# Attention and a feed-forward layer on one core: turned blocks written at the end of a slot, the product with v at its slot's end

## Chip, cores and metric

The kernel runs on one core of a Trainium2 chip. The metric is the device time of one execution in microseconds (us). Engines are named as the profile names them: PE (TensorE, matrix products), PEld (its weight loads), DVE (VectorE), ACT (ScalarE), POOL (GpSimd) and SP (SyncE, which here issues every transfer).

## Reference

8 batches, 8 heads, 576 positions, head size 64; model width 512. An attention with a decay on the scores, then a normalised feed-forward layer with a residual, all in float32:

```python
scores = scale * np.matmul(q, k.transpose(0, 1, 3, 2))
cum = np.cumsum(np.log(np.clip(f, 0.0001, 1.0)), axis=-1)
scores = np.where(causal, -1e9, scores + cum[:, :, :, None] - cum[:, :, None, :])
attn = np.exp(scores - scores.max(-1)); attn = attn / (attn.sum(-1) + 1e-9)
x = np.matmul(attn, v)                      # heads side by side: (8, 576, 512)
xn = (x - mu) / np.sqrt(var + 1e-6) * g_ln
out = x + np.maximum(xn @ w_ch1, 0.0) @ w_ch2
```

## The kernel before

**Two lanes of work, one list of slots.** The 64 heads are walked one after the other, each in four slots, one for each group of query rows: t = 1, 2, 3, 4 with 192, 320, 448 and 576 keys (the slot t = 1 also does the 64x64 corner, tile 0). I call them t1 to t4; the slot after t4 is t1 of the next head. In each slot, besides its attention work, one unit of the feed-forward layer runs: `mm1` (lines 691 to 693, twelve products into `h`) and `mm2` (lines 713 to 715, six products into `acc`, for the unit of the slot before). There are 288 such units; those that the slots do not hold run after the last head.

**Two forms of a head.** Heads 0 to 15 (`full`) are done with plain float32 products. Heads 16 to 63 split every operand in a high and a low part. Their probabilities must be transposed before the product with v, and this is done without PE. These are the pieces that matter here:

- `Q`, `S`, `e`, `B`: scores on PE (384, 385); score plus mask with the row minimum on DVE (425); exponential on ACT (436); on DVE the reciprocal of the row sum (441, 442) and on POOL the multiplication by it (443).
- `T`, one slot after the scores: `turn` transposes 32x32 blocks of the probabilities on DVE (461, 463) into a buffer `pb`. There is one `pb` for the whole kernel.
- `write` (471): in the slots t3 and t1 one transfer brings `pb` with two slots' blocks to DRAM (`pd`): 128x768 floats for query groups 1 and 2, 128x1152 for groups 3 and 4. Before the change it is issued right behind `T`.
- `V` (`read`, 482): in the slots t4 and t2 four transfers read `pd` back in the transposed order, into `pt`; one buffer for each of the two sizes.
- `H`, `G` (498, 502), `l` (506), `o` (513): in the slots t2 and t4, four slots after the scores, ACT copies the high part `ph`, DVE and POOL subtract it to get the low part; `o`, on POOL, overwrites `pt`.
- `A` (606): in the slots t1 and t3, PE multiplies both parts with `vv`. `F` (647) and `a` (658) bring the result to SBUF on ACT and DVE, and for every second head a transfer writes it to DRAM (660).
- `k`: in t1 the raw keys of the next head are split (ACT 342, POOL 345), in t3 its raw queries (ACT 350, POOL 356). Both come through one buffer `raw`, loaded by line 325. In a slot t1 the queries are loaded over the keys, and in a slot t3 the keys of the head behind them over the queries: each load waits until POOL has subtracted from the old content. In t3 `load_v` (332) follows it. `values_high` (362, DVE) and `values_low` (365, POOL) split v.

**What sets the order.** No scheduler: `ORDERS` (line 51) holds one letter for each piece, and the loop over the slots runs the pieces in the order of the letters. Each engine executes its instructions in the order in which they were issued, and so does SP with its transfers: a transfer that waits holds back all behind it. `M` and `N` are `mm1` and `mm2`, `m` the low part of their hidden values (704), `R` the loads and splits of the next token chunk, `D` the loads of raw q, k and v, `b` and `L` the small statistics of a chunk. A chunk of 256 tokens ends every 16 slots, with two transfers to the output (792).

Of the kernel before, what the change touches and what calls it, by code (L numbers as in the profile page):

```python
# [15 lines left out]
B, H, S, D = 8, 8, 576, 64  # L16
# [5 lines left out]
C = 256  # L22
# [27 lines left out]

ORDERS = [
    (0, "WwQsSthAeMrgFBmlLNPaRf"),
    (37, "WwkQSTstAMhPeHlgNFGrxfmBoVDLRba"),
    (66, "kQSTAHeVGFtlahBoMPrxmNbRLD"),
]


# [1 line left out]
def attn_moe(ctx: ExitStack, tc: tile.TileContext, qk, v, f, g, w1, w2, out):  # L59
# [304 lines left out]
    def values_low(h):  # L364
        nc.gpsimd.tensor_tensor(
            out=h.vv[:, :, 1, :], in0=h.vr, in1=h.vv[:, :, 0, :].bitcast(F32), op=ALU.subtract
        )
# [100 lines left out]
    def write(h, t):  # L468
        w = (6 if t == 2 else 9) * 32
        pd = dram.tile([P, 4 * w], F32, tag=f"pd{t}", bufs=2, name=f"pd{t}_{h.n}")  # L470
        nc.sync.dma_start(out=pd, in_=turned[0][:, : 4 * w])
        h.pd = getattr(h, "pd", {})
        h.pd[t] = pd
# [177 lines left out]
    def finish_add(h):  # L651
        po, w, c0 = h.o
        b, hh = divmod(h.n, H)
        pr, j = divmod(hh, 2)
        g1, xs = c0 == 0, h.xs
        js = slice(64 * j, 64 * j + 64)
        if not h.full:
            nc.vector.tensor_tensor(out=xs[js, :], in0=po[0:64, :w], in1=h.tmp[js, :w], op=ALU.add)  # L658
        if j == 1:
            nc.sync.dma_start(out=(xd1 if g1 else xd2)[b][P * pr : P * pr + P, :], in_=xs)  # L660
# [198 lines left out]

    slots = [(n, t) for n in range(B * H) for t in (1, 2, 3, 4)]  # L860
    nu = len(slots)
    slots += [None] * (DONE + 1)
    hd = {}

    def start_head(n):
# [12 lines left out]
    for u, slot in enumerate(slots):  # L878

        def before(k):  # L880
            return slots[u - k] if u >= k else None
# [5 lines left out]
        for back in (LAG + 1, DONE):  # L887
            if before(back) is not None and before(back)[1] in (2, 4) and hd[before(back)[0]].full == (back == LAG + 1):
                av, av_t = hd[before(back)[0]], before(back)[1]
        want = moe.can(wp.ready()) and u >= FIRST_MOE  # L890

        def tiles(h, t):
# [4 lines left out]
        def piece(c):  # L897
            tu = before(LAG)
            if tu is not None and not hd[tu[0]].full:
                tu = None  # L900
            late = before(HIGH)
            if late is not None and (hd[late[0]].full or late[1] in (1, 3)):
                late = None
            due_read = before(READ)
            if due_read is not None and (hd[due_read[0]].full or due_read[1] in (1, 3)):
                due_read = None
            past = before(1)
            if past is not None and hd[past[0]].full:
                past = None
            if c == "t" and tu is not None:  # L910
                transpose_unit(hd[tu[0]], tu[1])
            elif c == "h" and tu is not None:
                transposed_hi(hd[tu[0]], tu[1])
            elif c == "T" and past is not None:
                for i in [1, 0] if past[1] == 1 else [past[1]]:
                    turn(hd[past[0]], i)
                if past[1] in (2, 4):
                    write(hd[past[0]], past[1])
            elif c == "V" and due_read is not None:
                read(hd[due_read[0]], due_read[1])  # L920
            elif c == "H" and late is not None:
                high_first(hd[late[0]], late[1])
            elif c == "G" and late is not None:
                high_rest(hd[late[0]], late[1])
            elif c == "l" and late is not None:
                low_first(hd[late[0]], late[1])
            elif c == "k":
                two = before(2)
                if two is not None and two[1] == 4 and not hd[two[0]].full:
                    values_low(hd[two[0]])  # L930
                if slot is not None and n + 1 >= NFULL and n + 1 < B * H and t in (1, 3):
                    (keys_high if t == 1 else queries_high)(hd[n + 1])
                    (keys_low if t == 1 else queries_low)(hd[n + 1])
            elif c == "x" and slot is not None and n + 1 >= NFULL and n + 1 < B * H and t == 3:
                queries_copy(hd[n + 1])
            elif c == "o" and late is not None:
                low_rest(hd[late[0]], late[1])
            elif c == "Q" and slot is not None:
                for i in tiles(h, t):
                    qk_mm(h, i)  # L940
            elif c == "A" and av is not None:
                av_unit(av, av_t)
            elif c == "S" and slot is not None:
                for i in tiles(h, t):
                    softmax_a(h, i)
            elif c == "e" and slot is not None:
                for i in tiles(h, t):
                    softmax_e(h, i)
            elif c in FILL:
                wp.fill(FILL[c])  # L950
            elif c == "s":
                wp.sums()
                if u == LAG:
                    busy(WARM[2])
            elif c == "F" and av is not None:
                finish(av)
            elif c == "a" and av is not None:
                finish_add(av)
            elif c == "r" and want:
                moe.first_high()  # L960
            elif c == "R":
                moe.limit = min(NCHUNK, max(0, min(u - LAG - 1, max(4 * NFULL, u - DONE))) // (4 * H) * S // C)
                moe.rest()
            elif c == "b":
                rows_stats(moe.cur)
            elif c == "L":
                run_later(RSTD)
            elif c == "M" and want:
                moe.first()
            elif c == "B" and slot is not None:  # L970
                for i in tiles(h, t):
                    softmax_b(h, i)
            elif c == "m" and want:
                moe.first_low()
            elif c == "W":
                due = 1 + min(u, W_CHANGE) / W_SLOTS + max(0, u - W_CHANGE) * W_TICKS
                while not wp.done() and wp.tick_no <= due:
                    wp.tick()
            elif c == "N":
                moe.second()  # L980
            elif c == "P":
                prep()
            elif c == "D":
                next_raw()
# [23 lines left out]

        def prep():

            if before(1) is not None and before(1)[1] == 4 and not hd[before(1)[0]].full:
                values_high(hd[before(1)[0]])
            if slot is not None:
                if t == 1 and n + 1 < NFULL:
                    start_head(n + 1)
                if t == LAG + 1 and h.full:
                    load_v(hd[n + 1])
# [51 lines left out]
```

## Time and profile before

| | |
|---|---|
| Median of 3 runs | 1284.99 us (1283.32 to 1291.8) |
| The profiled execution | 1285.22 us, span 1283.2 us |
| Granted PE clock, mean | 0.987 |
| Busy share of the span | PE 90%, PEld 80%, DVE 60%, ACT 50%, POOL 46% |
| Transfers | 185.35 MB on SP's queue, 48.5% of 16 DMA engines' span |

The split heads fill the span from about 240 to 1070 us; then feed-forward units alone run until the end. A row of groups or of the timeline names the engine, the line, the tile written and the tiles read, and the shape; the number in brackets is the idle time of the engine ahead of it and what ended it. A row of the waits gives, for one engine and line, whom it waited for: us in total, how often, and the longest. `SPq` is SP's queue of transfers; its time for a transfer is that of issuing it, not of the transfer. A timeline of several engines is printed in order of time; where it was asked for one engine, rows of others are missing.

### The profile page before, as it was taken

To read this page: it belongs to the slowest core of one execution; us is meant where nothing else is said; L and a number is where in the kernel's file an instruction comes from. 1 tells how busy PE (TensorE), PEld (TensorE's weight loads), DVE (VectorE), ACT (ScalarE), POOL (GpSimd) and SP (SyncE) were. 2 spreads that over 40 slices of the span, in tenths; PEclk is the share of its full clock that TensorE was granted. 3 is DMA by queue.
4 is the path that set the end of the run, shared out by engine and by line. 5 is a ranking of instruction groups with operands and counts; after the bars stand their busy time and mean duration, and the time that the engine had idled before them with its cause. 6 is when DMAs were issued, how large, how long until landed. Compare 5 with 4: busy or idle time off the path is not lost. (4 is left out here: it accounts for less than half of the span.)

```text
span 1283.2 us, 24610 instructions
## 1 busy us (share of the span) xinstructions
PE 1159.3 (90%) x7648; PEld 1025.9 (80%) x7648; DVE 770.7 (60%) x2706; ACT 646.2 (50%) x1744; POOL 594.3 (46%) x870
## 2 busy tenths in 40 slices
PE   8889999888988888988888988889888889999998
PEld 6657888778887787878787878788787879999997
DVE  6777774576757576666667676766666672222222
ACT  6886665455555555545555555555455542111111
POOL 3454454465556565555655565655555541000000
PEclk9999999999999999999999999999999999999999
DMA  6555532656656555647565656556565642110100
GB/s 182 161 146 159 159 83 66 187 165 184 185 169 178 161 172 186 195 153 203 174 182 175 200 166 179 157 186 180 170 189 175 187 149 60 45 38 18 50 25 25
DMA packets 165169, 186.91 MB, mean 146 GB/s; under 512 B 45488, under 2 KB 131504, under 8 KB 165040
## 3 DMA queue, kind: packets, MB, share of 16 engines
q1 hardware_dynamic: 165040, 185.35, 48.5%
q8 instruction: 61, 1.00, 0.3%
q14 instruction: 68, 0.56, 0.2%
HBM read 118.93 MB, written 66.36 MB: 144 GB/s over the span
## 5 line engine op out<-in xcount | busy, mean ns | idle before, releaser
L443 POOL TENSOR_SCALAR p<-p,st 64x64 f32<-64x64 f32 (+4 forms) x320 | 169.6, 535 | 434.6 <-DVE st L442 196.7
L691 PE MATMUL h<-x,w1h 128*128 128x256 f32 x1152 | 336.0, 292 | 0.4 <-DVE st L425 0.4
L692 PE MATMUL h<-x,w1h 128*128 128x256 f32 x1152 | 328.8, 285 | 0.0
L693 PE MATMUL h<-x,w1l 128*128 128x256 f32 x1152 | 328.8, 285 | 0.0
L436 ACT ACTIVATE p<-p,st 64x64 f32<-64x64 f32 (+4 forms) x320 | 179.1, 560 | 264.4 <-DVE st L425 244.9
L704 DVE SCALAR_TENSOR_TENSOR hh<-h,hh 128x256 fp32r<-128x256 f32 x288 | 121.7, 422 | 229.1 <-ACT hh L699 227.5
L713 PE MATMUL acc<-w2h,hh 128*128 128x512 f32 x576 | 230.7, 401 | 0.0
L714 PE MATMUL acc<-w2l,hh 128*128 128x512 f32 x576 | 229.8, 399 | 0.0
L699 ACT ACTIVATE hh<-h 128x256 fp32r<-128x256 f32 x288 | 109.6, 380 | 237.7 <-PE h L693 236.1
L715 PE MATMUL acc<-w2h,hh 128*128 128x512 f32 x576 | 227.0, 394 | 0.0
L691 PEld LDWEIGHTS h<-x,w1h 128*128 128x128 f32 x1152 | 221.6, 192 | 5.5 <-issue 0.9
L692 PEld LDWEIGHTS h<-x,w1h 128*128 128x128 f32 x1152 | 222.9, 193 | 2.5
L693 PEld LDWEIGHTS h<-x,w1l 128*128 128x128 f32 x1152 | 223.1, 194 | 0.0
L425 DVE CUSTOM_DVE_ANT_0 p<-s,mask 64x64 f32<-64x64 f32 (+4 forms) x320 | 130.5, 422 | 82.4 <-PE s L385 76.6
L513 POOL TENSOR_TENSOR pt<-pt,ph 128x384 fp32r<-128x384 f32 x96 | 149.5, 1558 | 6.1 <-ACT ph L502 6.1
L606 PE MATMUL o<-pt,vv 128*64 128x256 f32 (+1 forms) x288 | 48.9, 278 | 101.4 <-POOL pt L513 97.8
L715 PEld LDWEIGHTS acc<-w2h,hh 128*128 128x128 f32 x576 | 109.7, 190 | 25.3
L713 PEld LDWEIGHTS acc<-w2h,hh 128*128 128x128 f32 x576 | 111.3, 193 | 14.5 <-ACT ph_full L568 0.2
L606 PEld LDWEIGHTS o<-pt,vv 128*64 128x64 f32 x288 | 29.6, 135 | 115.4 <-POOL pt L513 115.4
L714 PEld LDWEIGHTS acc<-w2l,hh 128*128 128x128 f32 x576 | 111.0, 193 | 12.0
L658 DVE TENSOR_TENSOR xs<-o,ot 64x320 f32<-64x320 f32 x96 | 43.2, 450 | 125.8 <-ACT ot L647 125.8
L776 POOL TENSOR_SCALAR sv<-sv 128x2 f32<-128x2 f32 x18 | 3.9, 215 | 188.9 <-DVE sv L760 187.7
(87 smaller groups left out, 2013.9 us busy)
## 6 DMA issues: line engine op xcount, KB each, us to landing
raw<-in_qk_dram SPq DMA_DIRECT2D x96, 288.0 KB
pd<-pb SPq DMA_DIRECT2D x48, 576.0 KB
pd<-pb SPq DMA_DIRECT2D x48, 384.0 KB
wr<-in_w_dram SPq DMA_DIRECT2D x32, 512.0 KB
pt<-pd SPq DMA_DIRECT2D x96, 144.0 KB
pt<-pd SPq DMA_DIRECT2D x96, 112.0 KB
vr<-in_v_dram SPq DMA_DIRECT2D x64, 160.0 KB
out_dram<-xt SPq DMA_DIRECT2D x36, 256.0 KB
```

The lines of the kernel that those rows point to most:

```text
L425: nc.vector.tensor_tensor_reduce(out=pt[:m, a:z], in0=sp, in1=mask[:m, off + a : off + z], scale=-SCALE, scalar=3.0e38 if i == 0 else st[: ...
L436: nc.scalar.activation(pt[:m, :w], pt[:m, :w], AF.Exp, bias=st[:m, i : i + 1], scale=-1.0, accum_out=st[:m, 2:3])
L443: nc.gpsimd.tensor_scalar(out=pt[:m, :w], in0=pt[:m, :w], scalar1=st[:m, 3:4], scalar2=1.0, op0=ALU.mult, op1=ALU.mult)
L513: nc.gpsimd.tensor_tensor(out=pt[:, :, z:, :], in0=pt[:, :, z:, :].bitcast(F32), in1=ph[:, :, z:, :].bitcast(F32), op=ALU.subtract)
L691: mm(ph, w1h[:, k, fs], c.x[k][:, 0, :], start=(k == 0), stop=False)
L692: mm(ph, w1h[:, k, fs], c.x[k][:, 1, :], start=False, stop=False)
L693: mm(ph, w1l[:, k, fs], c.x[k][:, 0, :], start=False, stop=(k == KT - 1))
L699: nc.scalar.activation(h[:, 0, :], c.ph, AF.Relu)
L704: nc.vector.scalar_tensor_tensor(out=h[:, 1, :], in0=ph, scalar=0.0, in1=h[:, 0, :].bitcast(F32), op0=ALU.max, op1=ALU.subtract)
L713: mm(c.acc[i], h[:, 0, ts_], w2h[:, j, :], start=(j == 0), stop=False)
L714: mm(c.acc[i], h[:, 0, ts_], w2l[:, j, :], start=False, stop=False)
L715: mm(c.acc[i], h[:, 1, ts_], w2h[:, j, :], start=False, stop=(j == FT - 1))
```

## The change

From slot 67 on (head 16, t4) the letters stand in another order, and three pieces move by a slot:

- The product with v, `A`, moves from behind the scores to the end of the slot, behind `M` and `N`. Its results `F` and `a` move to the next slot, so from t1 and t3 to t2 and t4 (`fin`).
- `V` moves from the middle of its slot to behind `D`.
- The write of `pb`, so far part of `T`, becomes a piece of its own, `d`, the last of the slot (the row of slot 37 has it too, since head 16's first slots fall under that row).
- v's split moves one slot: `values_high` from t1 to t2, `values_low` from t2 to t3. The limit of the feed-forward lane moves by a slot, and one empty slot is added at the end.

```diff
 ORDERS = [
     (0, "WwQsSthAeMrgFBmlLNPaRf"),
-    (37, "WwkQSTstAMhPeHlgNFGrxfmBoVDLRba"),
-    (66, "kQSTAHeVGFtlahBoMPrxmNbRLD"),
+    (37, "WwkQSTstAMhPeHlgNFGrxfmBoVDLRbad"),
+    (67, "kQSTHeGFtlahBoMNAPrxmbRLDVd"),
 ]
...
-    slots += [None] * (DONE + 1)
+    slots += [None] * (DONE + 2)
...
+        fin = av if av is not None and av.full else None
+        if before(DONE + 1) is not None and before(DONE + 1)[1] in (2, 4) and not hd[before(DONE + 1)[0]].full:
+            fin = hd[before(DONE + 1)[0]]
...
-                if past[1] in (2, 4):
-                    write(hd[past[0]], past[1])
+            elif c == "d" and past is not None and past[1] in (2, 4):
+                write(hd[past[0]], past[1])
...
-                two = before(2)
-                if two is not None and two[1] == 4 and not hd[two[0]].full:
-                    values_low(hd[two[0]])
+                three = before(3)
+                if three is not None and three[1] == 4 and not hd[three[0]].full:
+                    values_low(hd[three[0]])
...
-            elif c == "F" and av is not None:
-                finish(av)
-            elif c == "a" and av is not None:
-                finish_add(av)
+            elif c == "F" and fin is not None:
+                finish(fin)
+            elif c == "a" and fin is not None:
+                finish_add(fin)
...
-                moe.limit = min(NCHUNK, max(0, min(u - LAG - 1, max(4 * NFULL, u - DONE))) // (4 * H) * S // C)
+                moe.limit = min(NCHUNK, max(0, min(u - LAG - 1, max(4 * NFULL, u - DONE - 1))) // (4 * H) * S // C)
...
-            if before(1) is not None and before(1)[1] == 4 and not hd[before(1)[0]].full:
-                values_high(hd[before(1)[0]])
+            if before(2) is not None and before(2)[1] == 4 and not hd[before(2)[0]].full:
+                values_high(hd[before(2)[0]])
```

**PE in a slot t1**, before: the product with v (`o`, lines 606; `ph` the high part, `pt` the low one) stands between the scores `s` and the unit of the feed-forward layer.

```order
L384 MATMUL s_0_0_6328<-hi_6075 64x128
L385 MATMUL s_0_0_6328<-kl_6076,xq_2840 64x128
L606 MATMUL o_4_6340<-ph_29_6276,vv_6130 128x256 x4
L606 MATMUL o_4_6340<-ph_29_6276,vv_6130 128x128
L606 MATMUL o_4_6340<-pt_29_6161,vv_6130 64x256 x3
L606 MATMUL o_4_6340<-pt_29_6161,vv_6130 64x128
L691 MATMUL h_0_6362<-x_0_5897,w1h 128x256
```

After, in the same slot:

```order
L713 MATMUL acc_1_5492<-w2h,hh_15_6304 128x512
L714 MATMUL acc_1_5492<-w2l,hh_15_6304 128x512
L715 MATMUL acc_1_5492<-w2h,hh_15_6304 128x512
L606 MATMUL o_4_6369<-ph_29_6272,vv_6183 128x256 x4
L606 MATMUL o_4_6369<-ph_29_6272,vv_6183 128x128
L606 MATMUL o_4_6369<-pt_29_6199,vv_6183 64x256 x3
L606 MATMUL o_4_6369<-pt_29_6199,vv_6183 64x128
L384 MATMUL s_2_0_6386<-hi_6075 128x320
```

The 18 products of lines 691 to 715 now stand ahead of it, and the scores of the next slot behind it.

**SP's transfers from a slot t1 to the next slot t3**, before, with what each waits for (`DMAHW` and a number: the completion of an earlier transfer, eight counters that the transfers take in turn; an engine's name: an instruction of that engine):

```order
L471 DMA pd_30_6338<-pb 128x1152 [waits DMAHW2_49,DVE_49]
L660 DMA xb_158<-xs_320_6107 128x256 [waits DMAHW3_49,DVE_49]
L792 DMA out_dram<-xt_0_6068 128x512 [waits DMAHW4_49,DVE_49]
L792 DMA out_dram<-xt_1_6194 128x512 [waits DMAHW5_49,DVE_49]
L325 DMA raw_0_6390<-in_qk_dram 128x576 [waits DMAHW6_49,Pool_49]
L482 DMA pt_30_6405<-pd_30_6338 32x4x288 [waits DMAHW7_49,DMAHW2_49,PE_49]
L482 DMA pt_30_6405<-pd_30_6338 32x4x288 [waits DMAHW0_49]
L482 DMA pt_30_6405<-pd_30_6338 32x4x224 [waits DMAHW1_49]
L482 DMA pt_30_6405<-pd_30_6338 32x4x224
L471 DMA pd_31_6450<-pb 128x768 [waits DMAHW3_49,DVE_49]
L325 DMA raw_1_6489<-in_qk_dram 128x576 [waits DMAHW6_49,DMAHW4_49,Pool_49]
L332 DMA vr_6491<-in_v_dram 128x320 [waits DMAHW5_49]
```

After:

```order
L792 DMA out_dram<-xt_0_6063 128x512 [waits DMAHW2_49,DVE_49]
L792 DMA out_dram<-xt_1_6188 128x512 [waits DVE_49]
L325 DMA raw_0_6382<-in_qk_dram 128x576 [waits DMAHW4_49,Pool_49]
L471 DMA pd_30_6384<-pb 128x1152 [waits DMAHW5_49]
L660 DMA xb_158<-xs_320_6155 128x256 [waits DMAHW6_49,DVE_49]
L482 DMA pt_30_6434<-pd_30_6384 32x4x288 [waits DMAHW7_49,DMAHW5_49,PE_49]
L482 DMA pt_30_6434<-pd_30_6384 32x4x288 [waits DMAHW0_49]
L482 DMA pt_30_6434<-pd_30_6384 32x4x224 [waits DMAHW1_49]
L482 DMA pt_30_6434<-pd_30_6384 32x4x224 [waits DMAHW2_49]
L325 DMA raw_1_6483<-in_qk_dram 128x576 [waits DMAHW4_49,DMAHW3_49,Pool_49]
L332 DMA vr_6485<-in_v_dram 128x320 [waits DVE_49]
L471 DMA pd_31_6487<-pb 128x768 [waits DVE_49]
```

Each write of `pb` (471) stood ahead of the load of `raw` (325) in its slot and now stands behind it, in t3 behind the load of v too.

**DVE in a slot t2**, before (the 320-key query group; `p_1` and `p_1_177` are the probabilities of the slot before, which `T` turns into `pb`):

```order
L425 ISA p_2_6396,st_2_6397<-s_2_0_6393,mask 128x320 [waits PE_49]
L425 ISA st_2_6397 128x1
L461 STREAM_TRANSPOSE pb<-p_1_6331 128x2x32 [waits DMAHW2_49,Pool_49]
L463 STREAM_TRANSPOSE pb<-p_1_6331 128x4x32
L461 STREAM_TRANSPOSE pb<-p_1_177 64x2x32 [waits Pool_49]
L506 TENSOR_TENSOR ph_30_6402<-pt_30_6279,ph_30_6402 64x4x96 [waits DMAHW6_49,DMAHW5_49,Activation_49]
L441 TENSOR_SCALAR st_2_6397<-st_2_6397 128x1 [waits Activation_49]
```

After:

```order
L425 ISA p_2_6389,st_2_6390<-s_2_0_6386,mask 128x320 [waits PE_49]
L425 ISA st_2_6390 128x1
L461 STREAM_TRANSPOSE pb<-p_1_6331 128x2x32 [waits DMAHW5_49,Pool_49]
L463 STREAM_TRANSPOSE pb<-p_1_6331 128x4x32
L461 STREAM_TRANSPOSE pb<-p_1_177 64x2x32 [waits Pool_49]
L506 TENSOR_TENSOR ph_30_6395<-pt_30_6315,ph_30_6395 64x4x96 [waits DMAHW6_49,Activation_49]
L658 TENSOR_TENSOR xs_320_6155<-o_4_6369,ot_320_6399 64x256 [waits Activation_49]
L441 TENSOR_SCALAR st_2_6390<-st_2_6390 128x1
```

Before and after, the first transposition waits for the completion of the write of `pb` that was issued in the slot t1 (`DMAHW2` in the one, `DMAHW5` in the other), since it overwrites what that write reads. `a` (658) has come in ahead of the reciprocal's first step (441).

## The prediction

> **What bounds the kernel now.** I read the stretches of 50 us first. A row of the stretches gives the stretch, its length, then the busy time of PE, PEld, DVE, ACT and POOL with their instructions, the granted clock, the transfers' share and GB/s.
>
> ```profile
> 600.00:650.00 50.00, 43.29 (x288) 39.19 (x287) 34.23 (x124) 26.49 (x70) 30.46 (x44) 1.00 0.55 168
> 1100.00:1150.00 50.00, 50.00 (x327) 45.52 (x326) 11.65 (x27) 8.68 (x23) 2.75 (x14) 1.00 0.12 34
> ```
>
> PE is the bound, wholly so in the tail (50.00 of 50). Between 240 and 1070 us it idles 6.7 of 50 us at a clock of 1.00, so something else ends last there at some point of each slot. The waits name it:
>
> ```profile
> PE o L606 <- POOL pt L513: 97.8, 64, 2.5
> DVE xs L658 <- ACT ot L647: 125.8, 96, 3.8
> SPq L471 <- DVE pb L463: 266.5, 93, 6.2
> SPq L325 <- POOL kl L345: 31.9, 22, 5.6
> SPq L325 <- POOL hi L356: 31.1, 23, 2.2
> DVE pb L461 <- DMA pd<-pb: 3.5, 3, 2.2
> ```
>
> PE waits 97.8 us for POOL's low part `o` ahead of the product with v, nearly all that it idles in this stage. The lower four rows matter for the change. SP waits 266.5 us for the transposed blocks: it arrives early at each write of `pb`, and the write goes as soon as the blocks exist. Only behind it SP waits for POOL, to load `raw`. And DVE hardly ever waits for the write (3.5 us in all) when it transposes into `pb` again a slot later.
>
> One head without chunk work, from the timelines of single engines:
>
> ```profile
> 642.04 0.24 DVE L461 STREAM_TRANSPOSE pb<-p 128x64 f32<-128x64 f32 x1
> 643.74 0.53 POOL L443 TENSOR_SCALAR p<-p,st 128x320 f32<-128x320 f32 x1 [2.43 <-DMA pt<-pd]
> 644.24 1.01 POOL L513 TENSOR_TENSOR pt<-pt,ph 128x384 fp32r<-128x384 f32 x1
> 645.33 1.43 POOL L356 TENSOR_TENSOR hi<-raw,hi 64x576 fp32r<-64x576 f32 x1
> 646.01 0.34 SPq L471 DMA_DIRECT2D pd<-pb  x1
> 647.78 0.38 SPq L325 DMA_DIRECT2D raw<-in_qk_dram  x1
> 650.00 0.24 DVE L461 STREAM_TRANSPOSE pb<-p 128x64 f32<-128x64 f32 x1
> 651.70 0.75 POOL L443 TENSOR_SCALAR p<-p,st 128x576 f32<-128x576 f32 x1 [3.16 <-DVE st L442]
> 652.41 2.09 POOL L513 TENSOR_TENSOR pt<-pt,ph 128x896 fp32r<-128x896 f32 x1
> 653.73 0.34 SPq L471 DMA_DIRECT2D pd<-pb  x1
> 654.46 1.42 POOL L345 TENSOR_TENSOR kl<-raw,hi 64x576 fp32r<-64x576 f32 x1
> 657.64 0.38 SPq L325 DMA_DIRECT2D raw<-in_qk_dram  x1
> 658.83 0.23 DVE L461 STREAM_TRANSPOSE pb<-p 128x64 f32<-128x64 f32 x1
> ```
>
> The transpositions at 642.04 (t2), 650.00 (t4) and 658.83 (t2 of the next head) are the ones that overwrite blocks just written out. Each follows a write by 4 to 5 us (646.01 to 650.00, 653.73 to 658.83). The load of `raw` cannot go before POOL's subtraction ends: at 645.33 + 1.43 = 646.76, and at 654.46 + 1.42 = 655.88. Today a write does not care. After the change it stands behind that load.
>
> **The loop that the change closes.** In the new order this chain runs around each head: transposition in t2, on DVE its followers `l`, `a`, `B`; POOL's normalisation, `o`, `values_low`, queries subtracted; SP's loads of `raw` and v, then the write of `pb`; its landing; transposition in t4; `l`, `a`, `B`; POOL's normalisation, `o`, keys subtracted; load of `raw`; write; landing; transposition in t2. Every link is an instruction order or a wait that the orders show. A head cannot take less than the sum of the links, however fast PE is. Now to the links.
>
> *From t2's transposition to its write.* Today 646.76 - 642.04 = 4.72 us to the end of POOL's subtraction. Two pieces come in: `a` ahead of `B` on DVE, and `values_low` on POOL ahead of the queries. Then the two loads are issued.
>
> ```profile
> L658 DVE TENSOR_TENSOR xs<-o,ot 64x320 f32<-64x320 f32 x48 | 23.2, 483 | 62.6 <-ACT ot L647 62.6
> L658 DVE TENSOR_TENSOR xs<-o,ot 64x256 f32<-64x256 f32 x48 | 20.0, 417 | 63.3 <-ACT ot L647 63.3
> L365 POOL TENSOR_TENSOR vv<-vr,vv 128x320 fp32r<-128x320 f32 x48 | 42.1, 878 | 2.3 <-issue 2.3
> L325 SPq DMA_DIRECT2D raw<-in_qk_dram x89: 332/376/662, 252.4 to 1023.9; - x89
> L332 SPq DMA_DIRECT2D vr<-in_v_dram x46: 377/426/1657, 262.8 to 1048.7; - x46
> ```
>
> 4.72 + 0.42 + 0.88 + 0.38 + 0.43 = 6.83 us.
>
> *From t4's transposition to its write.* 655.88 - 650.00 = 5.88, plus `a` 0.48 and one load 0.38: 6.74 us.
>
> *Landing.* No view gives it directly; I bound it by who waits behind a write:
>
> ```profile
> 602.64 0.34 SPq L471 DMA_DIRECT2D pd<-pb  x1
> 603.80 0.35 SPq L325 DMA_DIRECT2D raw<-in_qk_dram  x1
> 605.50 2.93 SPq L482 DMA_DIRECT2D pt<-pd  x4
> 819.97 0.34 SPq L471 DMA_DIRECT2D pd<-pb  x1
> 824.57 0.24 DVE L461 STREAM_TRANSPOSE pb<-p 128x64 f32<-128x64 f32 x1 [0.59 <-DMA pd<-pb]
> 926.42 0.34 SPq L471 DMA_DIRECT2D pd<-pb  x1
> 929.17 1.79 SPq L482 DMA_DIRECT2D pt<-pd  x4
> ```
>
> The wide write (t1, 576 KB) of 602.64 let the reading behind it go at 605.50, after SP had stood idle: 2.86 us. After the change 288 KB of `raw` are in the queue just ahead. How fast the queue moves bytes, from its packets, MB and share of the 16 engines' span:
>
> ```profile
> q1 hardware_dynamic: 165040, 185.35, 48.5%
> ```
>
> At 185.35 MB in 48.5% of 1283.2 us, 298 GB/s, `raw` is 1.0 us, of which 0.4 pass while it is issued. Bounds 2.86 and 3.5; I take 3.1, between. The narrow write (t3, 384 KB) had landed 2.75 us after 926.42; by its bytes it can be 0.66 us shorter than the wide one, 2.2; but the one of 819.97 held DVE until 824.57, 4.6 us. Bounds 2.2 and 4.6; with `raw` and v ahead of it I take 2.75, nearer to the quick rows, which are the many: DVE waited only three times.
>
> The Trainium skill (DMA: Bandwidth & Descriptors, section Anatomy of one DMA — SWDGE (gpsimd) path) fits a transfer as about 2.0 us, mostly the receipt of the write at its target, plus its bytes at 436 GB/s. By that estimate the writes take 3.35 and 2.90 us, and the sum below gains 0.4 us a head, 18 us in all. The trace's 2.86 for the wide one is shorter, and these writes are issued by SP, not GpSimd, so the trace's values stand; the rule agrees that some 2 us go by however little is written, which speaks against putting a write on a chain.
>
> *Sum:* 6.83 + 2.75 + 6.74 + 3.1 = 19.42 us for a head without chunk work.
>
> *Chunk work on the loop.* Every fourth head POOL does the small statistics between `o` and the subtraction, and SP two output transfers ahead of `raw`:
>
> ```profile
> 610.37 0.21 POOL L776 TENSOR_SCALAR sv<-sv 128x2 f32<-128x2 f32 x1
> 611.78 0.20 POOL L784 TENSOR_TENSOR rs<-rs 128x2 f32<-128x2 f32 x1
> 624.20 1.00 SPq L792 DMA_DIRECT2D out_dram<-xt  x2
> ```
>
> Six such operations take 611.98 - 610.37 = 1.6 us; with a second, shorter series in t4 and part of the 1.0 us on SP I estimate 2.8 us in four heads, 0.7 a head. Other chunk work on DVE falls into its waiting. So 20.1 us a head. Today's mean period:
>
> ```profile
> 237.08 0.51 DVE L506 TENSOR_TENSOR ph<-pt,ph 64x384 fp32r<-64x384 f32 x1
> 1060.68 0.55 DVE L506 TENSOR_TENSOR ph<-pt,ph 64x384 fp32r<-64x384 f32 x1
> L506 DVE TENSOR_TENSOR ph<-pt,ph 64x384 fp32r<-64x384 f32 x48 | 24.5, 510 | 0.0
> ```
>
> (1060.68 - 237.08) / 47 = 17.52 us. The loop is closed from head 17 until the loads of `raw` end with head 62, 46 periods: 46 x (20.1 - 17.52) = 119 us longer.
>
> **The other parts, at nothing.** *`A` at the end of its slot:* PE's 97.8 us of waiting go, since 18 products of the feed-forward layer now cover `o`; but PE then waits for the loop, through the hidden values of line 704 and the scores' banks, which DVE serves only after the transposition that waits. Behind that transposition stand, on DVE, `l`, `a`, `B`, v's cast and the hidden values' low part, and behind those POOL's normalisation and PE's `mm2`. Without the loop this is the 97.8 us of the first rival. *`F` and `a` a slot later:* DVE's 125.8 us of waiting for them go the same way; their own durations are on the loop above. *`V` behind `D`:* in t2 and t4 `D` loads nothing; `V` waits for the write anyway, then issues for 1.8 us (929.17) and lands, by the writes' bound, at most 4.6 us later. `H` needs it two slots on, 9.6 us by the sum: hidden by 3 us. *The empty slot and the later limit:* at most one feed-forward unit, 18 products of the 327 in the tail's 50 us, 2.75 us; nothing expected, since the units run one a slot as before. The units left for the tail do not change, so nothing is given back there.
>
> **Forecast.** The profiled execution's 1285.22 (span 1283.2; the median of the runs is 1284.99, so no correction) plus 119 makes 1404 us. Bounds: quick landings and no chunk work, 6.83 + 2.2 + 6.74 + 2.86 = 18.63, 46 x 1.11 = 51, 1336 us; slow ones, 6.83 + 4.6 + 6.74 + 3.5 + 0.7 = 22.37, 46 x 4.85 = 223, 1508 us.
>
> **Rivals.**
>
> *PE's wait goes and nothing takes its place* (faster). The product with v has its operands, DVE no longer waits for `a`, and PE closes up: 1285.2 - 97.8 = 1187 us, 17.52 - 97.8/47 = 15.4 us a head. For it: the 97.8 us are PE's only large wait, and no engine's busy time reaches 15.4 us a head besides. Against it: it needs a loop under 15.4, and the POOL and SP links alone cannot be passed. It decides if the write's position does not matter, for instance because POOL runs far enough ahead.
>
> *The gain pays the loss* (no change). The loop is some 2.5 us shorter than I count, so that the period stays at 17.5: 1285 us. It takes landings well under 2 us; no row shows one.
>
> *Only the wide write bites.* The narrow one lands before t4's transposition, whose slack is longest (646.76 to 650.00), so only the second half stretches: from 658.83 - 650.00 = 8.83 to 6.74 + 3.1 = 9.84 us. 46 x 1.01 = 46: 1331 us. Against it: `a` and `values_low` eat 1.3 us of that slack.
>
> **Chances.** Forecast 0.74, with its own bounds; only one write 0.08; no change 0.06; faster 0.12. A measurement of this kernel tells about 1% from no change: slower by more 0.82, within 0.06, faster by more 0.12. The range 1325 to 1500 holds the forecast's bounds but their upper end, and the third rival; the other two, 0.18, are left out.
>
> **What will show it.** Right: DVE's line 461 waits for `pd<-pb` some 90 times, 200 to 330 us in all (DVE works 34.23 of 50 us, 12.0 of 17.5 a head; of the other 8.1 x 46 = 373 us the greater part); SP waits for POOL ahead of line 325 far beyond today's 63 us, and hardly for DVE's blocks ahead of line 471; PE's wait of line 606 is near nothing while PE's busy share falls from 90% to about 82% (its 1159 us in 1404); from one t2 to the next 20 us. Wrong: a wait of line 461 under 50 us, or writes of `pb` that are issued before POOL's subtraction ends, or a head in under 18 us.

## The result and the profile after

The changed kernel takes 1546.28 us (median of 4 runs, 1541.27 to 1547.38) against 1284.49 us: a ratio of 1.202, with an interval from 1.198 to 1.207. Slower was forecast, but at 1404 us, and the range ended at 1500.

The waits of the profile after; the first five answer to the waits of lines 461, 325 and 606 shown of before:

```profile
DVE pb L461 <- DMA pd<-pb: 366.8, 95, 6.2
SPq L325 <- POOL hi L356: 138.2, 38, 5.7
SPq L325 <- POOL kl L345: 98.1, 29, 5.6
PE o L606 <- POOL pt L513: 26.9, 31, 0.9
PE o L606 <- POOL vv L365: 35.9, 29, 2.3
PE acc L715 <- DVE hh L704: 162.7, 68, 5.1
POOL p L443 <- DVE st L442: 559.4, 102, 8.4
```

DVE, which waited 3.5 us for the writes of `pb`, now waits 366.8 us, nearly every time. SP's wait for POOL ahead of the load of `raw` has grown from 63 to 236 us, and the write stands behind it. PE's wait for `o` is down from 97.8 to 26.9 us, as the change meant, but the same product now waits another 35.9 us for v's low part, which the change made a slot later, and PE waits 162.7 us for the hidden values, which DVE serves behind the transposition that waits. The chain that ended last, by engine and then by line:

```profile
PE 34%; DMA 26%; DVE 16%; POOL 12%; issue 7%; ACT 2%; SPq 2%; POOLq 0%; DVEq 0%; ACTq 0%
DMA pd<-pb 24%; POOL pt L513 5%; PE acc L715 4%; PE o L606 4%; PE acc L713 4%; PE acc L714 4%; PE h L691 3%; PE h L692 3%; PE h L693 3%; DVE xs L658 2%; DVE pb L463 2%; DVE ph L506 2%; DVE p L425 2%; PE s L382 2%; POOL kl L345 2%
```

24% of the span is the landing of writes of `pb`. It stands first of all lines, ahead of POOL's product `pt` with 5%. One head, from the timelines of the single engines:

```profile
703.54 0.24 DVE L461 STREAM_TRANSPOSE pb<-p 128x64 f32<-128x64 f32 x1 [5.05 <-DMA pd<-pb]
706.19 1.24 POOL L513 TENSOR_TENSOR pt<-pt,ph 128x384 fp32r<-128x384 f32 x1
707.39 0.87 POOL L365 TENSOR_TENSOR vv<-vr,vv 128x320 fp32r<-128x320 f32 x1
708.34 1.41 POOL L356 TENSOR_TENSOR hi<-raw,hi 64x576 fp32r<-64x576 f32 x1
709.78 0.35 SPq L325 DMA_DIRECT2D raw<-in_qk_dram  x1
710.18 0.42 SPq L332 DMA_DIRECT2D vr<-in_v_dram  x1
710.70 0.38 SPq L471 DMA_DIRECT2D pd<-pb  x1
715.37 0.24 DVE L461 STREAM_TRANSPOSE pb<-p 128x64 f32<-128x64 f32 x1 [3.88 <-DMA pd<-pb]
718.14 2.12 POOL L513 TENSOR_TENSOR pt<-pt,ph 128x896 fp32r<-128x896 f32 x1
720.20 1.42 POOL L345 TENSOR_TENSOR kl<-raw,hi 64x576 fp32r<-64x576 f32 x1
721.65 0.35 SPq L325 DMA_DIRECT2D raw<-in_qk_dram  x1
722.09 0.38 SPq L471 DMA_DIRECT2D pd<-pb  x1
726.40 0.24 DVE L461 STREAM_TRANSPOSE pb<-p 128x64 f32<-128x64 f32 x1 [4.24 <-DMA pd<-pb]
```

This is the forecast's loop, link by link and without a gap: POOL's subtraction ends at 709.75, `raw` goes at 709.78, the write at 710.70, the transposition when it has landed, at 715.37; then the same again with the keys. What differs is the landings: 4.67 and 4.31 us, where the sum had 2.75 and 3.1. The whole stage, from the first and the last subtraction `l` in a slot t2:

```profile
242.01 0.51 DVE L506 TENSOR_TENSOR ph<-pt,ph 64x384 fp32r<-64x384 f32 x1
1320.49 1.27 DVE L506 TENSOR_TENSOR ph<-pt,ph 64x384 fp32r<-64x384 f32 x1
```

(1320.49 - 242.01) / 47 = 22.95 us a head, against 17.52 before. 47 x 5.43 = 255 us, which with 6 us outside the stage is the 261 us between the two spans.

### The profile page after: what moved, and what is told of

It is laid out like the page before. It is cut to its first block, busy times and chain, and to the rows that moved or that the text cites. A ratio compares the mean times of both kernels' runs of the same rounds, so it can differ in the third digit from the quotient of the medians.

```text
span 1544.5 us, 24448 instructions
## 1 busy us (share of the span) xinstructions
PE 1280.4 (83%) x7648; PEld 1106.4 (72%) x7648; DVE 742.4 (48%) x2706; ACT 653.9 (42%) x1744; POOL 599.7 (39%) x870
## 4 chain that ended last, share of the span: by engine, by line
PE 34%; DMA 26%; DVE 16%; POOL 12%; issue 7%; ACT 2%; SPq 2%; POOLq 0%; DVEq 0%; ACTq 0%
DMA pd<-pb 24%; POOL pt L513 5%; PE acc L715 4%; PE o L606 4%; PE acc L713 4%; PE acc L714 4%; PE h L691 3%; PE h L692 3%; PE h L693 3%; DVE xs L658 2%; DVE pb L463 2%; DVE ph L506 2%; DVE p L425 2%; PE s L382 2%; POOL kl L345 2%
## 5 line engine op out<-in xcount | busy, mean ns | idle before, releaser
L715 PE MATMUL acc<-w2h,hh 128*128 128x512 f32 x576 | 248.0, 431 | 162.9 <-DVE hh L704 162.7
L692 PE MATMUL h<-x,w1h 128*128 128x256 f32 x1152 | 343.3, 298 | 18.9 <-DVE x L676 18.9
L691 PE MATMUL h<-x,w1h 128*128 128x256 f32 x1152 | 346.9, 301 | 0.4 <-DVE st L425 0.4
L693 PE MATMUL h<-x,w1l 128*128 128x256 f32 x1152 | 339.4, 295 | 0.0
L715 PEld LDWEIGHTS acc<-w2h,hh 128*128 128x128 f32 x576 | 115.6, 201 | 218.5 <-DVE hh L704 194.6
L692 PEld LDWEIGHTS h<-x,w1h 128*128 128x128 f32 x1152 | 236.4, 205 | 26.6 <-DVE x L676 23.4
L691 PEld LDWEIGHTS h<-x,w1h 128*128 128x128 f32 x1152 | 237.4, 206 | 5.8 <-issue 0.9
L461 DVE STREAM_TRANSPOSE pb<-p 128x64 f32<-128x64 f32 (+1 forms) x240 | 58.0, 242 | 374.4 <-DMA pd<-pb 366.8
L713 PE MATMUL acc<-w2h,hh 128*128 128x512 f32 x576 | 237.7, 413 | 0.0
L693 PEld LDWEIGHTS h<-x,w1l 128*128 128x128 f32 x1152 | 235.6, 205 | 0.0
L713 PEld LDWEIGHTS acc<-w2h,hh 128*128 128x128 f32 x576 | 115.8, 201 | 11.1 <-ACT ph_full L568 0.2
L606 PEld LDWEIGHTS o<-ph,vv 128*128 128x128 f32 x384 | 74.8, 238 | 64.6 <-POOL vv L365 59.9
L606 PE MATMUL o<-ph,vv 128*128 128x256 f32 (+2 forms) x384 | 80.6, 342 | 35.9 <-POOL vv L365 35.9
L384 PE MATMUL s<-hi 128*128 128x288 f32 (+4 forms) x288 | 101.0, 360 | 0.0
```

Of the source, the lines that this page charges most:

```text
L606: mm(o.rearrange("p (r a i) -> p r a i", a=4, i=32), st, view(x).rearrange("p a r i -> p r a i"), start=first, stop=True, skip_group_check ...
L691: mm(ph, w1h[:, k, fs], c.x[k][:, 0, :], start=(k == 0), stop=False)
L692: mm(ph, w1h[:, k, fs], c.x[k][:, 1, :], start=False, stop=False)
L693: mm(ph, w1l[:, k, fs], c.x[k][:, 0, :], start=False, stop=(k == KT - 1))
L713: mm(c.acc[i], h[:, 0, ts_], w2h[:, j, :], start=(j == 0), stop=False)
L715: mm(c.acc[i], h[:, 1, ts_], w2h[:, j, :], start=False, stop=(j == FT - 1))
```

## The experiments

Theory: the loop through the load of `raw`, the landing of the write and the reuse of `pb` is the whole loss, and the other parts of the change are a gain. Rivals: the late product and its followers cost, or the late blocks themselves; and, for the size, what makes a landing long. Ratios are to the kernel before, run on the same chip. "Landing" is worked out from each kernel's timelines as the time from the issue of a write (471) to the start of a transposition (461) that waited for it, median where nothing else is said. The ways from t2 to t4 and from t4 to t2 are means over 45 heads, from the first transposition of one slot to that of the other.

### The write alone, in both directions

The changed kernel with the write back behind the transposition:

```diff
                 for i in [1, 0] if past[1] == 1 else [past[1]]:
                     turn(hd[past[0]], i)
+                if past[1] in (2, 4):
+                    write(hd[past[0]], past[1])
...
-            elif c == "d" and past is not None and past[1] in (2, 4):
-                write(hd[past[0]], past[1])
```

> The changed kernel with one part undone: the write of pb goes again right behind the transposition, so ahead of the load of raw; the late product with v, the late reads and v's later split stay. Theory (the loop through raw's load and the write's landing): DVE's wait for the write at line 461, 366.8 us in the changed kernel, falls under 20 us, the period of a head falls from 22.9 us to between 15.4 (PE alone) and 16.5 us, and the time to 1187 to 1240 us, below the kernel before. Rival (the late product, its results a slot later or v's later split are what costs): still over 1400 us.

Measured: 1239.5 us, ratio 0.963 (0.959 to 0.966), so 1239.5 - 1546.3 = 307 us below the changed kernel. A head takes 16.47 us. The theory held but for one number: DVE still waits for the write 46.5 us, not under 20.

The kernel before with only the write moved:

```diff
-    (37, "WwkQSTstAMhPeHlgNFGrxfmBoVDLRba"),
-    (66, "kQSTAHeVGFtlahBoMPrxmNbRLD"),
+    (37, "WwkQSTstAMhPeHlgNFGrxfmBoVDLRbad"),
+    (66, "kQSTAHeVGFtlahBoMPrxmNbRLDd"),
...
-                if past[1] in (2, 4):
-                    write(hd[past[0]], past[1])
+            elif c == "d" and past is not None and past[1] in (2, 4):
+                write(hd[past[0]], past[1])
```

> The kernel before with one part of the change alone: the write of pb as the last transfer of its slot, behind the load of raw; product with v, its results and v's split where they were. Theory (loop): the links without a and values_low, 4.72 + 0.9 + 3.6 to 4.0 (landing, as the changed kernel's trace has it) and 5.88 + 0.48 + 4.4 to 4.6, with 0.7 for chunk work, give 20.7 to 21.3 us a head in place of 17.5, so 1285 + 46 x 3.2 to 3.8 = 1430 to 1460 us, with DVE waiting some 90 times for the write. Rival (the write alone is harmless): 1285 us.

Measured: 1544.99 us, ratio 1.201 (1.194 to 1.208), 22.8 us a head. The move of the write alone costs as much as the whole change, but not by the same path. It is more than the links that I had summed, 1430 to 1460 us, and DVE waits for the write 74 times, not some 90, and half as long as in the changed kernel:

```profile
DVE pb L461 <- DMA pd<-pb: 175.2, 74, 5.6
PE o L606 <- POOL pt L513: 161.4, 94, 3.0
PE o L606 <- DVE ph L506: 95.8, 44, 4.2
```

With the product with v still in the middle of the slot, PE waits 257 us for its operands, and what comes behind it holds up SP. From the timelines of single engines, a head whose chunk ends there:

```profile
640.82 0.80 PE L606 MATMUL o<-ph,vv 128*128 128x256 f32 x5 [1.82 <-DVE ph L506]
642.30 2.24 POOL L513 TENSOR_TENSOR pt<-pt,ph 128x896 fp32r<-128x896 f32 x1
644.59 1.01 PE L606 MATMUL o<-pt,vv 128*64 128x256 f32 x4 [2.97 <-POOL pt L513]
646.53 0.34 SPq L660 DMA_DIRECT2D xb<-xs  x1
650.44 1.54 SPq L792 DMA_DIRECT2D out_dram<-xt  x2
652.07 0.38 SPq L325 DMA_DIRECT2D raw<-in_qk_dram  x1
652.50 0.44 SPq L471 DMA_DIRECT2D pd<-pb  x1
656.93 0.25 DVE L461 STREAM_TRANSPOSE pb<-p 128x64 f32<-128x64 f32 x1 [4.92 <-DMA pd<-pb]
```

`o` lets the product go at 644.59; the attention result's transfer (646.53) and the output (650.44) need what comes out of PE behind it, and the load of `raw` and the write stand behind them on SP. From t4 to t2 it takes 12.8 us, against 11.8 in the changed kernel; from the end of POOL's subtraction to the write 2.3 of them, against 0.7. From t2 to t4 it takes 10.1 us, against 11.4; to the end of POOL's subtraction 5.2 of them, against 6.4, which is about what the sum had for `a` and `values_low` (0.42 + 0.88). So the late product shortens one half of the loop, and these two lengthen the other by about as much.

### Reuse of the buffer, or late blocks

The changed kernel without the transpositions that come first after a write:

```diff
                 for i in [1, 0] if past[1] == 1 else [past[1]]:
-                    turn(hd[past[0]], i)
+                    if past[1] in (2, 4):
+                        turn(hd[past[0]], i)
```

> The changed kernel, with the transpositions left out that come first after a write, those of query groups 1 (with the corner) and 3; their blocks in pb stay zero, so the product with v lacks these groups. Writes, loads, reads and all else stand as in the changed kernel, and DVE has 1.4 us less work a head. If the loss is DVE's wait to overwrite pb: the loop is open and the time falls to that of the variant with the write behind the transposition, 1225 to 1265 us, although the writes land as late as before. If it is the late blocks themselves (the reads of pd, and with them the copies on ACT): over 1400 us.

Measured: 1270.69 us, ratio 0.988 (0.983 to 0.993). Without the reuse of `pb` a slot after its write, the time is 276 us below the changed kernel's, more than the whole loss of 262 us, though the write stands where the change put it. It ends 6 us above the expected bound, and the waits name why:

```profile
ACT ph L498 <- DMA pt<-pd: 165.4, 85, 4.2
DVE pb L461 <- DMA pd<-pb: 49.1, 47, 3.4
```

ACT now waits for blocks that come back late. So the late blocks do cost: with what DVE still waits they make up the 31 us to the variant with the early write; the reuse costs the rest. DVE had some 1.4 us less work a head here, so 31 us may be a little low. A second buffer `pb` would open the loop without leaving blocks out; no run has it.

### Only one of the two writes

```diff
                     turn(hd[past[0]], i)
+                if past[1] == 2:
+                    write(hd[past[0]], past[1])
...
-            elif c == "d" and past is not None and past[1] in (2, 4):
+            elif c == "d" and past is not None and past[1] == 4:
                 write(hd[past[0]], past[1])
```

> The changed kernel with only the wide write (slot t1) behind the load of raw; the narrow one (slot t3) goes right behind its transposition. The links from t4's transposition to t2's stay, 6.57 + 0.9 + 4.58 = 12.05 us by the changed kernel's means; the way from t2 to t4 is free and takes what it takes with both writes early, some 7 to 8.2 us. So 19.1 to 20.3 us a head in place of 16.5, and 1360 to 1415 us. Rival (a loop needs both waits; DVE's idle time absorbs one): under 1265 us.

Measured: 1444.51 us, ratio 1.123 (1.118 to 1.128), 30 us above the range. The split was right: t2 to t4 takes 8.0 us, as with both writes early (7.9), and t4 to t2 13.0 us, 0.9 more than the sum of its links; 20.86 us a head. The excess lies ahead of the write: to the end of POOL's subtraction 7.7 us pass, close to the 7.5 with both writes early, where the changed kernel has 6.57. DVE waits for `pd<-pb` 51 times, 215.7 us. One write behind the load costs 205 us over the variant with none, the second another 102. So a single wait is not absorbed.

### Behind the loads, or merely late

```diff
-    (67, "kQSTHeGFtlahBoMNAPrxmbRLDVd"),
+    (67, "kQSTHeGFtlahBoMNAPrxmbRLdDV"),
```

> The changed kernel with the write still in the last part of its slot, behind the output's and the token chunk's transfers, but ahead of the loads of raw and v (two letters exchanged, the reads of pd last). Theory (it is the load of raw, which waits for POOL, that the write must not stand behind): within 2% of the variant with the write right behind the transposition, 1187 to 1250 us. Rival (the end of the slot itself is too late): over 1350 us.

Measured: 1329.68 us, ratio 1.033 (1.029 to 1.038): between the two. Out of the load's shadow the write is worth 217 us, but the end of the slot still costs 90 us over the place behind the transposition. It hits the heads with chunk work: of DVE's 121.4 us of waiting for the write, by the timelines, 46 us (12 waits) follow a write that stood right behind the output's transfers and 71 us (25 waits) one right behind the chunk's loads. One of the first kind, from the timelines of SP and DVE:

```profile
713.43 1.02 SPq L792 DMA_DIRECT2D out_dram<-xt  x2
714.50 0.44 SPq L471 DMA_DIRECT2D pd<-pb  x1
719.75 0.24 DVE L461 STREAM_TRANSPOSE pb<-p 128x64 f32<-128x64 f32 x1 [4.95 <-DMA pd<-pb]
```

Here the write stood behind the output's two transfers, which wait for the end of the chunk on PE and DVE. Neither of my two cases had room for this; what I had named the cause, the load, is the largest of the things that the write must not stand behind, not the only one.

### How long a write takes to land

The load of `raw` was cut in two, with its first columns ahead of the write (they wait for POOL as the whole load did), the rest and v behind it. A new piece `E`, last in the order, issues what was left back. First with 16 columns:

```diff
-    (37, "WwkQSTstAMhPeHlgNFGrxfmBoVDLRbad"),
-    (67, "kQSTHeGFtlahBoMNAPrxmbRLDVd"),
+    (37, "WwkQSTstAMhPeHlgNFGrxfmBoVDLRbadE"),
+    (67, "kQSTHeGFtlahBoMNAPrxmbRLDVdE"),
...
-        nc.sync.dma_start(out=h.raw, in_=qk[h.n][:, i, :])
+        nc.sync.dma_start(out=h.raw[:, 0:16], in_=qk[h.n][:, i, 0:16])
+        rest_of.append(lambda: nc.sync.dma_start(out=h.raw[:, 16:S], in_=qk[h.n][:, i, 16:S]))
...
-                load_v(h)
+                rest_of.append(lambda: load_v(h))
...
+            elif c == "E":
+                while rest_of:
+                    rest_of.pop(0)()
```

> The changed kernel with the load of raw cut in two: its first 16 columns, which wait for POOL as the whole did, stay ahead of the write, the other 560 columns and the load of v go behind it. So the write waits for POOL as in the changed kernel, but with next to no bytes just ahead of it. If bytes ahead in the queue made the landing 4.4 and 3.6 us (median) in place of 2.9 and under 2.8: landings fall to 2.9 and 2.8, a head takes some 19.6 us and the kernel 1385 to 1405 us. If the landing is as long without them (the reads run beside it, or the write is slow by itself at this place): 1525 to 1546 us, only v's issue of 0.4 us a head gained.

Measured: 1437.22 us, ratio 1.117 (1.111 to 1.123): 109 us gained, 32 to 52 short of the range, 20.74 us a head; the narrow landing fell to 2.86 us as expected, the wide one to 3.37 only, not to 2.9. Then with 288 columns:

```diff
-        nc.sync.dma_start(out=h.raw[:, 0:16], in_=qk[h.n][:, i, 0:16])
-        rest_of.append(lambda: nc.sync.dma_start(out=h.raw[:, 16:S], in_=qk[h.n][:, i, 16:S]))
+        nc.sync.dma_start(out=h.raw[:, 0:288], in_=qk[h.n][:, i, 0:288])
+        rest_of.append(lambda: nc.sync.dma_start(out=h.raw[:, 288:S], in_=qk[h.n][:, i, 288:S]))
```

> As the variant with the loads cut in two, but with half of raw (288 columns, 144 KB) ahead of the write in place of 16. If the bytes ahead set the landing, it lies half way: wide (t1) 3.9 us median between 3.4 (16 columns) and 4.4 (all), narrow (t3) about 3.1 between 2.9 and 3.6; the period 21.4 to 21.9 us and 1470 to 1500 us. If it is not the bytes but the number of transfers or the place: the landings of one of the two ends, and 1437 or 1526 us.

Measured: 1449.29 us, ratio 1.125 (1.115 to 1.136), 21 us below the range, and 20.98 us a head; against the kernel with 16 columns, 136 KB more ahead cost 12 us, and the remaining 144 KB, with v, 97. Last with 16 columns ahead, and the rest a slot later, behind the reads of `pd`:

```diff
-    (37, "WwkQSTstAMhPeHlgNFGrxfmBoVDLRbadE"),
-    (67, "kQSTHeGFtlahBoMNAPrxmbRLDVdE"),
+    (37, "WwkQSTstAMhPeHlgNFGrxfmBoVDLRbaEd"),
+    (67, "kQSTHeGFtlahBoMNAPrxmbRLDVEd"),
...
-            elif c == "E":
+            elif c == "E" and (slot is None or t in (2, 4)):
```

> As the variant with 16 columns of raw ahead of the write, but the other 560 columns and v a slot later, behind the reads of pd, so that nothing large follows the write closely. Only the landing is asked: if the loads right behind the write still slowed it (wide 3.4 us there, 2.86 in the kernel before at 602.64), it is now 2.8 to 3.0 us, narrow 2.2 to 2.8. If not: 3.4 and 2.9 again. The time depends on what the later raw holds up, ACT's split of the queries above all; 1390 to 1460 us, with no weight in the verdict.

Measured: 1587.71 us in one execution, far above the range; the late `raw` holds up the split of the queries (from t2's transposition to the end of POOL's subtraction 8.7 us on the mean in place of 6.4), which says nothing on the landing. Medians of the landings that DVE waited for, some 45 of each kind:

| ahead of the write | behind it | narrow, 384 KB | wide, 576 KB |
|---|---|---|---|
| 16 columns of raw | nothing large | 2.51 | 2.97 |
| 16 columns of raw | 560 columns (and v) | 2.86 | 3.37 |
| 288 columns of raw | 288 columns (and v) | 3.03 | 3.47 |
| all of raw (and v): the change | nothing large | 3.54 | 4.38 |

One wide landing of the first row and one of the last, from the timelines of SP and DVE; the first kernel:

```profile
665.78 0.45 SPq L476 DMA_DIRECT2D pd<-pb  x1
668.76 0.24 DVE L466 STREAM_TRANSPOSE pb<-p 128x64 f32<-128x64 f32 x1 [3.15 <-DMA pd<-pb]
```

and the changed one:

```profile
654.65 0.44 SPq L471 DMA_DIRECT2D pd<-pb  x1
659.21 0.24 DVE L461 STREAM_TRANSPOSE pb<-p 128x64 f32<-128x64 f32 x1 [4.75 <-DMA pd<-pb]
```

With nothing large near them, the two landings differ by 0.46 us for 192 KB, some 430 GB/s, over a fixed 1.6 us (2.97 - 576 KB / 430 GB/s); two points give this line, so it is an estimate. All of `raw` ahead adds 1.41 us to the wide one, `raw` and v 1.03 to the narrow one. It is not in proportion: half of `raw` ahead was to lie half way and lies nearer to the low end (3.47 between 3.37 and 4.38, 3.03 between 2.86 and 3.54). What is shown is that the loads next to the write lengthen it, those ahead of it most.

The traces also keep each packet of a transfer with its size (4608 bytes for the wide write, 2304 for the whole `raw`), and these say where the 1.41 us go. Medians of the 47 wide landings of each kernel, in us from the issue of the write:

| ahead of the write | raw: first packet starts | raw: last one done | write: first starts | write: last done | DVE goes on |
|---|---|---|---|---|---|
| 16 columns of raw | 0.51 | 0.96 | 0.88 | 2.52 | 2.97 |
| all of raw: the change | 0.54 | 2.47 | 1.81 | 3.94 | 4.38 |

`raw` is issued 0.44 us before the write, and when the write is issued no packet of `raw` has moved yet. Its packets then take 1.9 us; the write's start 0.93 us later than behind 16 columns and take 0.5 us longer.

Some landings are 1 to 2 us longer than others with the same neighbours. In the changed kernel the narrow writes of 548.98 and 595.00 each had `raw` and v right ahead and nothing behind, and took 4.88 and 3.47 us. The queues in the two stretches from write to transposition, with packets, MB and share (548.9 to 553.9, then 594.9 to 598.5):

```profile
q1 hardware_dynamic: 432, 0.85, 50.6%
q8 instruction: 1, 0.02, 1.1%
```

```profile
q1 hardware_dynamic: 432, 0.85, 72.4%
```

In the long one there is one more packet, 16 KB of the kind that the profile calls instruction, and the last packets of the write are done after it. Of the 95 landings in the changed kernel 32 have such a packet, of 8 or 16 KB, in them; their medians are 4.77 us (narrow) and 4.58 (wide), those of the others 3.50 and 4.32. In the kernel of the first row the landings without one lie between 2.43 and 2.70 and between 2.90 and 3.07 us; those with one reach 4.44 and 5.32. Not each such packet lengthens a landing, and in the changed kernel some long ones have none. No run moves these packets, so that they are the cause is not shown.

### Reads back in the middle of the slot

On top of the variant with the early write:

```diff
-    (67, "kQSTHeGFtlahBoMNAPrxmbRLDVd"),
+    (67, "kQSTHeVGFtlahBoMNAPrxmbRLD"),
```

> The variant with the write behind the transposition (1239.5 us), and the reads of pd back in the middle of their slot, ahead of the attention result's transfer and the token chunk's loads, as in the kernel before. That variant still waits 46.6 us, 45 times, at line 461 for a write that was held up on SP behind what stands ahead of the reads. If that is what is left: under 15 us of such waits, and 1210 to 1232 us, the fastest of all so far. If the reads' place is of no weight: 1236 to 1243 us.

Measured: 1223.91 us, ratio 0.952 (0.949 to 0.956), the fastest of all.

```profile
DVE pb L461 <- DMA pd<-pb: 15.6, 23, 2.6
PE o L606 <- POOL vv L365: 18.7, 25, 2.3
PE o L606 <- POOL pt L513: 18.1, 35, 0.9
```

DVE's wait for the write is 15.6 us, just above the 15 expected. What is left of PE's waiting for the product with v is 37 us, half of it for v's low part, which the change made a slot later. A head takes 16.15 us.

## Why the prediction was right in kind and short in size

*What bounds the kernel, and PE's 97.8 us:* right in the main. With the writes early, the rest of the change brings 3.7%, and 4.8% with the reads back in their place; there the profile loses 61 of the 97.8 us of that wait. That the wait goes to nothing was wrong: in the changed kernel 62.8 us are left at line 606, 35.9 of them for v's low part, whose later place the prediction did not price.

*The loop:* right. The signs of the path came: line 461 waited 95 times (some 90), SP waited for POOL ahead of line 325, and hardly for DVE ahead of line 471. The sizes did not: the transpositions' wait was 366.8 us, beyond the 200 to 330, and a head took 22.95 us, not 20. That PE's busy share fell to 83% (82%) is luck: the forecast had 1159 us busy in 1404, the profile has 1280 in 1544, at a granted clock of 0.90 on the mean instead of 0.99.

*The legs:* right. From t2's transposition to the end of POOL's subtraction 6.36 us on the mean and from t4's 6.57, together 12.9; the sum had 4.72 + 0.42 + 0.88 and 5.88 + 0.48, and 0.7 for chunk work, together 13.1. Short was the way from there to the write: 1.02 and 0.73 us on the mean, where the sum had 0.81 and 0.38, so 0.56 us a head, 26 us in 46 heads.

*The landing:* this step failed. "Bounds 2.86 and 3.5; I take 3.1" for the wide write, and "with `raw` and v ahead of it I take 2.75" for the narrow one. They took 4.51 and 3.99 us on the mean, the outputs' and chunks' transfers included. That is 1.41 + 1.24 = 2.65 us a head, 122 us in 46 heads, of the 142 us by which the time was missed. By the medians, 4.38 and 3.54 us, it is 2.07 us a head; the rest is the single long landings. The rows that I measured by came from writes that stood first in the queue, and I priced the bytes ahead as a drain at the queue's mean rate, 0.6 us for the wide write, since 0.4 of 1.0 us were to pass while `raw` is issued; the cut loads show 1.41. By the packets, none of `raw` moves in that time, and its packets take 1.9 us, not 1.0. The choice of the quick rows for the narrow one, because "DVE waited only three times", was wrong in the same way: those were the rows before the change, in which no load stood ahead. The same rows had a narrow landing of 4.6 us (819.97), which was set aside; it has an instruction packet in it, as have the other two for which DVE waited before, and so have a third of those after. The wide write's upper bound, 3.5 us, failed too; the narrow one's bounds, 2.2 to 4.6, held. With the slow bounds the sum gave 1508 us, so the range could not hold 1546.

The Trainium skill (DMA: Bandwidth & Descriptors, section Anatomy of one DMA — SWDGE (gpsimd) path) gave an estimate of 3.35 and 2.90 us for the two. With nothing large near them, the runs show 2.97 and 2.51 on SP's queue: its slope agrees (some 430 against 436 GB/s), its fixed 2.0 us is 1.6 here. The rest came with the neighbours, and for those ahead the same page of the Trainium skill has a rule (section Queues, rings and completion order): the count that reports a transfer as done is written only after all earlier writes of the same DMA engine have landed. The runs agree in sign, with 1.41 and 1.03 us from the loads ahead, but do not show that rule at work: by the packets the write's own bytes move later, which is enough for all of the 1.41 us. That loads behind add 0.35 and 0.40 us is not covered by it either, and at 430 GB/s the 288 KB of `raw` are 0.69 us, half of what they added ahead of the wide write.

*The other parts at nothing:* half right. `V` behind `D` was put at nothing; with the loop gone it costs 1239.5 - 1223.9 = 16 us, because the attention result's transfer and the chunk's loads ahead of it wait, and the next write stands behind it. The blocks read back were to be hidden by 3 us; the copies `ph` wait 27.0 us for them in the changed kernel and 0.6 us with the reads in the middle of the slot and the write early. The late product is a gain only without the loop, as said.

*The rivals:* "only the wide write bites" had the right way from t4 to t2, but the run with that order gave 1444.5, not 1331: by the landing (4.5 us, not 3.1) and as much by the way to the write (8.4, not 6.74). The faster rival lacked the place of the write above all; with it early the time is 1239.5 and 1223.9 us, not 1187.

## What to carry to other kernels

A transfer on a queue that keeps its order takes over the waits of all that stands ahead of it, and whoever reuses its source takes them over too; look for the next writer of the source buffer before a write is moved back. Price a landing from rows in which it stood where it will stand: behind which loads, and with what right behind it. A move of several pieces should be timed piece by piece, since here the write's letter turned a gain of 3.7% into a loss of 20%.

## What the hardware showed that I had not expected

The granted clock of PE was lower where PE idled more: between 400 and 900 us it was 0.98 in the kernel before, 0.87 in the changed one, 1.00 in the fastest variant. The rows give the stretch, its length, the busy time of PE, PEld, DVE, ACT and POOL, then the clock, of before, the changed kernel and the variant with writes and reads early:

```profile
400.00:900.00 500.00, 438.74 (x2842) 396.36 (x2840) 336.81 (x1205) 270.23 (x697) 288.00 (x390) 0.98 0.59 178
```

```profile
400.00:900.00 500.00, 386.45 (x2155) 336.40 (x2155) 242.05 (x912) 208.39 (x528) 217.55 (x285) 0.87 0.46 137
```

```profile
400.00:900.00 500.00, 471.02 (x3092) 422.62 (x3091) 342.08 (x1316) 295.39 (x758) 314.50 (x409) 1.00 0.64 193
```

PE's busy time in the changed kernel therefore looks larger than its work: 0.18 us a product (386.45 us for 2155), against 0.15 before. The total of idle time does not give the clock by itself: in the same stretch it was 0.91 in the kernel with 16 columns ahead, with PE busy 411 us, and 0.86 in the one with only the wide write last, with 413. In the changed kernel the mean hides stretches at half the clock. Here is one, right behind a wait, and the stretch that follows it:

```profile
569.26 0.54 PE L715 MATMUL acc<-w2h,hh 128*128 128x512 f32 x1 [3.52 <-DVE hh L704]
569.60:573.00 3.40, 3.40 (x13) 2.61 (x11) 1.29 (x8) 1.99 (x5) 3.22 (x4) 0.50 0.64 156
573.00:590.10 17.10, 13.25 (x87) 11.51 (x86) 7.66 (x32) 7.11 (x18) 5.12 (x6) 1.00 0.45 137
```

The Trainium skill (TensorE: Matmul & The Clock Gate, Part 1) says that the clock is throttled when PE has been idle for long; with this wait of 3.52 us and others of up to 5.1 us ahead of line 715 the trace agrees. The forecast's loop has no PE link, so the clock should not have set most of the changed kernel's time. But PE's product `o` does stand in the chain that ended last, with 4% of the span, and no run here holds the clock fixed to show it.
